# A depthwise-separable layer with k = 1: weights loaded in halves, a wait for each scaled slice, dummy matmuls, and a last store issued by two engines

## The chip, the core and the metric

The kernel runs on one core of a Trainium2 chip. The core has TensorE (matmuls into PSUM), VectorE, ScalarE, GpSimd and SyncE, and 16 DMA engines that move data between HBM and SBUF. In the profile they are called PE (with PEld for the loads of the stationary operand), DVE, ACT, POOL and SP; SPq and ACTq are the queues from which SyncE and ScalarE issue DMAs. The metric is device time in microseconds for one execution. About 0.2% can be told from no change.

## What is computed

```python
x: (1, 384, 384, 384), dw: (1, 1, 384), pw: (384, 384)      # bfloat16
out = x * dw[0, 0][None, None, None, :]                      # k = 1, pad = 0
return jnp.einsum('bhwc,cd->bhwd', out, pw)
```

With k = 1 the depthwise step is one factor for each channel. The kernel moves it into the weights: row c of pw is multiplied by dw[c] once, and all else is one matmul of 147,456 rows of 384 channels by a 384 x 384 matrix. x and the output are 113 MB each.

## The kernel before, in words

**Tiling.** Rows go through in 288 supertiles of 512. Supertiles are grouped in 76 chunks: 1, 1, 2, then 70 chunks of 4, then 2, 1, 1. A chunk of x is one load into one of four buffers X (1.5 MB for four supertiles); its output is one store from one of four buffers O. There are two buffers T for transposed data and two in PSUM (PS), for even and odd supertiles.

**One supertile.** VectorE transposes it from X to T with two 32-bit STREAM_TRANSPOSEs (line 174), half h = 0 for the channel blocks b = 0 to 2, h = 1 for b = 3 to 5. TensorE then runs 48 matmuls (line 134): six blocks b, two parities par, four row groups q of 32 rows each, which work side by side in the array; four matmuls with the same b and par make a "step". Each reads the scaled weights w_r of its slice (b, par) and accumulates into bank q. VectorE evicts bank 3 (line 212) and ScalarE banks 0 to 2 (line 215) to O as bfloat16, and VectorE transposes the supertile after the next.

**What sets the order.** Everything is written out by hand, with semaphores. Each engine runs its own instructions in order.

- SyncE issues, one after the other: the first x load, two loads of pw, the x loads of chunks 1 to 3; then in a loop over chunks t the load of chunk t + 4 (line 95; it waits until chunk t is transposed) and the store of chunk t (lines 105 and 107; they wait for both evictions). At the end it waits for all stores (line 125).
- ScalarE issues the load of dw and the two other loads of pw (line 89), loads its activation table, makes two tiny copies (line 160) that set s_a for the first turn, and then scales.
- pw is loaded four times, once into each group of 32 partitions: 288 KB each, 1.15 MB in all. dw becomes dwsel, one float factor for each partition, by four small copies on VectorE (line 186).
- Scaling: twelve slices (b, r) of 128 x 384; VectorE takes r = 0 (line 197), ScalarE r = 1 (line 199). Both wait for all four loads of pw. All twelve increment s_wr, and TensorE waits for twelve before its loop:

```python
        nc.tensor.wait_ge(s_wr, 2 * NB)
        with nc.tensor.Fori(0, NS // 2, 1) as it:
            rv = nc.tensor.to_reg(it + 1)
            for s in range(2):
                supertile(s, rv)
```

- The loop on TensorE is a hardware loop of 144 turns with two supertiles in its body. Inside, the first matmul of b = 0 and of b = 3 waits for the transposes (s_t), and matmuls of b = 0 wait for the evictions of the supertile that used this PSUM buffer (s_a at q = 0, s_d at q = 3).
- VectorE's order at the start is: seeds of s_d, dwsel, the transposes of supertile 0, its six slices, the transposes of supertile 1, then the loop of evictions and transposes.

Of the kernel before, what the change touches and what calls it, by code (L numbers as in the profile page):

```python
# [7 lines left out]
BF16 = mybir.dt.bfloat16  # L8
F32 = mybir.dt.float32
U32 = mybir.dt.uint32  # L10
COPY = mybir.ActivationFunctionType.Copy
# [3 lines left out]
NO = 4  # L15
# [11 lines left out]
def kernel(  # L27
# [11 lines left out]
    nc = tc.nc  # L39
    P = nc.NUM_PARTITIONS  # L40
    B, H, W, C = x.shape
    assert dw.shape[0] == 1 and dw.shape[1] == 1, "only k=1 depthwise supported"
    D = pw.shape[1]
    N = B * H * W
    assert C == 384 and D == 384 and N % 1024 == 0
    NB = C // 64

    xf = x.rearrange("b h w c -> (b h w) c")
    of = out.rearrange("b h w d -> (b h w) d")

    NS = N // 512
    chunks = _chunks(NS)
    NT = len(chunks)
    s0 = [sum(chunks[:t]) for t in range(NT)]

    consts = ctx.enter_context(tc.tile_pool(name="consts", bufs=1))
# [3 lines left out]
    pw_r = consts.tile([P, NB, 2, D], BF16, name="pw_r")  # L60
    w_r = consts.tile([P, NB, 2, D], BF16, name="w_r")
    dwt = consts.tile([32, NB, 2], BF16, name="dwt")
    dwsel = consts.tile([P, NB * 2], F32, name="dwsel")
    warm = consts.tile([P, 3], F32, name="warm")
    seed = consts.tile([P, 2], F32, name="seed")

    Xs = [bufp.tile([P, 4 * LMAX, C], BF16, name=f"X{i}") for i in range(NX)]
    Ts = [bufp.tile([P, NB, 256], BF16, name=f"T{i}") for i in range(2)]
    Os = [bufp.tile([P, 4 * LMAX * D], BF16, name=f"O{i}") for i in range(NO)]
    PS = [psum.tile([P, 4, 512], F32, name=f"ps{s}") for s in range(2)]  # L70
# [4 lines left out]
    s_a = [nc.alloc_semaphore(f"s_a{i}") for i in range(2)]  # L75
    s_d = [nc.alloc_semaphore(f"s_d{i}") for i in range(2)]
    s_o = [nc.alloc_semaphore(f"s_o{i}") for i in range(NO)]
    s_dw = nc.alloc_semaphore("s_dw")
    s_pw = nc.alloc_semaphore("s_pw")
    s_ds = nc.alloc_semaphore("s_ds")  # L80
    s_wr = nc.alloc_semaphore("s_wr")
    s_seed = nc.alloc_semaphore("s_seed")

    with tc.tile_critical():  # L84
        pw_v = pw.rearrange("(b w r) d -> w b (r d)", w=32, r=2)
        dw_v = dw.rearrange("a e (b w r) -> w (a e b) r", w=32, r=2)

        def load_pw(eng, q):
            eng.dma_start(pw_r[32 * q : 32 * q + 32].rearrange("w b r d -> w b (r d)"), pw_v).then_inc(s_pw, 16)  # L89

        def load_x(t):
            L = chunks[t]
            r = 512 * s0[t]
            src = xf[r : r + 512 * L, :].rearrange("(p s) c -> p (s c)", p=P)
            d = nc.sync.dma_start(Xs[t % NX][:, : 4 * L, :].rearrange("p s c -> p (s c)"), src)  # L95
            if t >= NX:
                je = s0[t - NX] + chunks[t - NX] - 1
                d._wait_ge(s_t[je % 2][1], je // 2 + 1)
            d.then_inc(s_x[t % NX], 16)

        def store(t):
            L = chunks[t]
            r = 512 * s0[t]
            je = s0[t] + L - 1
            nc.sync.wait_ge(s_d[je % 2], je // 2 + 2)
            dst = of[r : r + 512 * L, :].rearrange("(q p j) d -> p q (j d)", q=4, p=P)
            d = nc.sync.dma_start(dst, Os[t % NO][:, : 4 * L * D].rearrange("p (q e) -> p q e", q=4))
            d._wait_ge(s_a[je % 2], je // 2 + 2)
            d.then_inc(s_o[t % NO], 16)


        nc.scalar.dma_start(dwt[:], dw_v).then_inc(s_dw, 16)
        load_x(0)
        load_pw(nc.scalar, 2)
        load_pw(nc.sync, 0)
        load_pw(nc.scalar, 3)
        load_pw(nc.sync, 1)
        for t in range(1, NX):
            load_x(t)
        for t in range(NT):  # L120
            if t + NX < NT:
                load_x(t + NX)
            store(t)
        for o in range(NO):
            nc.sync.wait_ge(s_o[o], 16 * len(range(o, NT, NO)))


        def supertile(s, rv):
            for b in range(NB):
                for par in range(2):  # L130
                    for q in range(4):
                        if par == 0 and q == 0 and b in (0, 3):
                            nc.tensor.wait_ge(s_t[s][b // 3], rv)
                        mm = nc.tensor.matmul(  # L134
                            PS[s][:, q, :D],
                            lhsT=Ts[s][32 * q : 32 * q + 32, b, par::2],
                            rhs=w_r[32 * q : 32 * q + 32, b, par, :],
                            start=(b == 0 and par == 0),
                            stop=(b == NB - 1 and par == 1),
                            tile_position=(32 * q, 0),  # L140
                        )
                        if b == 0 and par == 0 and q == 0:
                            mm._wait_ge(s_a[s], rv)
                        elif b == 0 and par == 0 and q == 3:
                            mm._wait_ge(s_d[s], rv)
                        if b in (2, 5) and par == 1 and q == 3:
                            mm.then_inc(s_pe)

        nc.tensor.wait_ge(s_wr, 2 * NB)
        with nc.tensor.Fori(0, NS // 2, 1) as it:  # L150
            rv = nc.tensor.to_reg(it + 1)
            for s in range(2):
                supertile(s, rv)


        for s in range(2):
            nc.vector.memset(seed[:, s : s + 1], 0.0).then_inc(s_d[s])  # L157
        nc.gpsimd.memset(warm[:], 0.0).then_inc(s_seed)  # L158
        for s in range(2):
            c = nc.scalar.copy(warm[:, s + 1 : s + 2], warm[:, 0:1])  # L160
            if s == 0:
                c._wait_ge(s_seed, 1)
            c.then_inc(s_a[s])

        def transposes(t, j):
            jj = s0[t] + j
            L = chunks[t]
            s = jj % 2
            Xw = Xs[t % NX][:].bitcast(U32)[:, : 4 * L, :].rearrange("p (k l) c -> p k l c", l=L)
            Tw = Ts[s][:].bitcast(U32).rearrange("p b (i k) -> p b k i", k=4)  # L170
            for h in range(2):
                if h == 0 and j == 0:
                    nc.vector.wait_ge(s_x[t % NX], 16 * (t // NX + 1))
                ins = nc.vector.transpose(  # L174
                    out=Tw[:, 3 * h : 3 * h + 3],
                    in_=Xw[:, :, j, 96 * h : 96 * h + 96].rearrange("p k (b w) -> p b k w", w=32),
                )
                if jj >= 2:
                    ins._wait_ge(s_pe, 2 * (jj - 2) + h + 1)
                ins.then_inc(s_t[s][h])  # L180

        order = [(t, j) for t in range(NT) for j in range(chunks[t])]

        nc.vector.wait_ge(s_dw, 16)
        for q in range(4):
            nc.vector.tensor_copy(  # L186
                dwsel[32 * q : 32 * q + 32, :], dwt[:].rearrange("w b r -> w (b r)")
            ).then_inc(s_ds)
        transposes(*order[0])
        for b in range(NB):  # L190
            for r in range(2):
                eng = nc.vector if r == 0 else nc.scalar
                if b == 0:
                    eng.wait_ge(s_pw, 64)  # L194
                sc = dwsel[:, 2 * b + r : 2 * b + r + 1]
                if r == 0:
                    i = nc.vector.tensor_scalar_mul(w_r[:, b, r, :], pw_r[:, b, r, :], sc)  # L197
                else:
                    i = nc.scalar.activation(w_r[:, b, r, :], pw_r[:, b, r, :], COPY, scale=sc)  # L199
                if b == 0:  # L200
                    i._wait_ge(s_ds, 4)
                i.then_inc(s_wr)
        transposes(*order[1])

        for jj, (t, j) in enumerate(order):
            L = chunks[t]
            s = jj % 2
            Ov = Os[t % NO][:, : 4 * L * D].rearrange("p (q j d) -> p q j d", q=4, d=D)
            if j == 0 and t >= NO:
                nc.vector.wait_ge(s_o[t % NO], 16 * (t // NO))  # L210
                nc.scalar.wait_ge(s_o[t % NO], 16 * (t // NO))
            e = nc.vector.tensor_copy(Ov[:, 3, j, :], PS[s][:, 3, :D])  # L212
            e._wait_ge(s_pe, 2 * jj + 2)
            e.then_inc(s_d[s])
            a = nc.scalar.copy(Ov[:, 0:3, j, :], PS[s][:, 0:3, :D])  # L215
            a._wait_ge(s_pe, 2 * jj + 2)
            a.then_inc(s_a[s])
            if jj + 2 < NS:
                transposes(*order[jj + 2])


# [28 lines left out]
```

## Time and profile before

| | us |
|---|---|
| median of 9 runs (lowest, highest) | 587.65 (586.56, 588.87) |
| the profiled execution's own time | 587.25 |
| its span, first to last instruction | 585.5 |
| TensorE busy (L134), 13,824 matmuls | 564.2 |
| VectorE busy | 564.1 |
| ScalarE busy | 327.1 |
| DMA: 227.8 MB, mean rate over the span | 389 GB/s |

The costliest groups of instructions are below. The columns are line, engine, operation, output<-input, shapes, count, then busy us in all, mean ns of one, idle us of the engine just before them, and what ended most of it.

```profile
L134 PE MATMUL ps<-w_r,T 32*128 32x384 bf16 x13824 | 564.2, 322 | 12.8 <-ACT w_r L199 12.8
L215 ACT CAST O<-ps 128x1152 bf16<-128x1152 f32 x288 | 322.4, 1120 | 243.3 <-PE ps L134 243.3
L174 DVE STREAM_TRANSPOSE T<-X 128x384 uint32<-128x384 uint32 x576 | 448.7, 853 | 0.0
L212 DVE CAST O<-ps 128x384 bf16<-128x384 f32 x288 | 160.7, 558 | 6.4 <-PE ps L134 6.4
L199 ACT ACTIVATE w_r<-pw_r,dwsel 128x384 bf16<-128x384 bf16 x6 | 3.1, 601 | 5.4 <-DMA pw_r<-in_pw_dram 5.4
```

Four matmuls of a step overlap, so the mean of 322 ns is not the time between steps: a supertile takes 1.95 us, a step 0.1625 us. TensorE, VectorE and the DMA engines are all busy nearly throughout, and the page's shares don't tell which of them ends last. A time in a window is counted from the start of the span; in the windows' rows the numbers are the stretch, its length, busy us (and instructions) of PE, PEld, DVE, ACT and POOL, TensorE's granted clock, the mean busy share of the 16 DMA engines, and GB/s.

### The profile page before, as it was taken

Reading aid. Unit: us, or ns where it says so; the run is one execution under the profiler, and the core shown is the slowest. Engines: PE = TensorE matmul, PEld = TensorE weight load, DVE = VectorE, ACT = ScalarE, POOL = GpSimd, SP = SyncE. Lnnn points to the kernel's source line nnn. Section 1 sums busy time; section 2 is a strip of 40 time slices with the busy share of each in tenths; the row PEclk is TensorE's granted clock in tenths of the full one; section 3 lists DMA queues with packets and bytes.
Section 4 is the critical chain, followed back from the end, with each engine's and each line's share of the span. In section 5 each row is a group of like instructions: output and inputs, shape, how many; then the busy total and the mean of one; then the engine's idle time right before and its main releaser. Section 6 shows DMA issues by size and latency. Waiting matters only on the chain.

```text
span 585.5 us, 30055 instructions
## 1 busy us (share of the span) xinstructions
PE 564.2 (96%) x13824; PEld 385.4 (66%) x13824; DVE 564.1 (96%) x876; ACT 327.1 (56%) x297; POOL 0.3 (0%) x5
## 2 busy tenths in 40 slices
PE   1999999999999999999999999999999999999994
PEld 0666666666666666666666666666666666666662
DVE  3899999999999999999999999999999999999993
ACT  3455555555555555555555555555555555555553
POOL 0000000000000000000000000000000000000000
PEclk9999999999999999999999999999999999999998
DMA  8999999999999999999999999999999999999966
GB/s 296 344 410 408 409 400 383 401 406 418 404 396 389 394 418 419 400 403 400 404 397 401 411 407 399 391 412 413 401 384 404 405 401 400 401 401 399 374 239 223
DMA packets 52126, 227.81 MB, mean 389 GB/s; under 512 B 2704, under 2 KB 6544, under 8 KB 43152
## 3 DMA queue, kind: packets, MB, share of 16 engines
q1 hardware_dynamic: 51488, 227.09, 98.5%
q10 hardware_dynamic: 624, 0.59, 0.4%
q14 instruction: 13, 0.11, 0.0%
q8 instruction: 1, 0.02, 0.0%
HBM read 114.43 MB, written 113.25 MB: 389 GB/s over the span
## 4 chain that ended last, share of the span: by engine, by line
PE 96%; DMA 1%; ACT 1%; SPq 0%; issue 0%; ACTq 0%
PE ps L134 96%; DMA pw_r<-in_pw_dram 1%; ACT w_r L199 1%; ACT O L215 0%; SPq L89 0%; SPq L95 0%; SPq L245 0%; ACTq L194 0%; SPq L84 0%
## 5 line engine op out<-in xcount | busy, mean ns | idle before, releaser
L134 PE MATMUL ps<-w_r,T 32*128 32x384 bf16 x13824 | 564.2, 322 | 12.8 <-ACT w_r L199 12.8
L134 PEld LDWEIGHTS ps<-w_r,T 32*128 32x128 bf16 x13824 | 385.4, 93 | 191.2 <-issue 12.8
L215 ACT CAST O<-ps 128x1152 bf16<-128x1152 f32 x288 | 322.4, 1120 | 243.3 <-PE ps L134 243.3
L174 DVE STREAM_TRANSPOSE T<-X 128x384 uint32<-128x384 uint32 x576 | 448.7, 853 | 0.0
L212 DVE CAST O<-ps 128x384 bf16<-128x384 f32 x288 | 160.7, 558 | 6.4 <-PE ps L134 6.4
L199 ACT ACTIVATE w_r<-pw_r,dwsel 128x384 bf16<-128x384 bf16 x6 | 3.1, 601 | 5.4 <-DMA pw_r<-in_pw_dram 5.4
L186 DVE CAST dwsel<-dwt 32x12 f32<-32x12 bf16 x4 | 0.7, 163 | 3.5 <-DMA dwt<-in_dw_dram 3.4
L197 DVE TENSOR_SCALAR w_r<-pw_r,dwsel 128x384 bf16<-128x384 bf16 x6 | 1.5, 313 | 2.5 <-DMA pw_r<-in_pw_dram 2.5
L160 ACT ACT_TABLE_LOAD x1 | 1.3, 1283 | 2.3 <-issue 2.3
L157 DVE MEMSET seed<- 128x1 f32 x2 | 0.1, 59 | 1.0 <-SPq L84 1.0
L160 ACT COPY warm<-warm 128x1 f32<-128x1 f32 x2 | 0.3, 188 | 0.0
L234 POOL MEMSET const-bfloat16-1.0<- 128x1 bf16 x1 | 0.1, 102 | 0.0
L234 POOL MEMSET const-uint8-127<- 128x1 uint8 x1 | 0.1, 102 | 0.0
L158 POOL MEMSET warm<- 128x3 f32 x1 | 0.1, 101 | 0.5 <-SPq L84 0.5
L234 POOL MEMSET const-float32-1.0<- 128x1 f32 x1 | 0.1, 100 | 0.0
L234 POOL MEMSET const-float32-0.0<- 128x1 f32 x1 | 0.1, 99 | 0.2 <-issue 0.2
## 6 DMA issues: line engine op xcount, KB each, us to landing
X<-in_x_dram SPq DMA_DIRECT2D x70, 1536.0 KB, 13.0
out_dram<-O SPq DMA_DIRECT2D x70, 1536.0 KB, 14.5
X<-in_x_dram SPq DMA_DIRECT2D x4, 384.0 KB, 10.0
X<-in_x_dram SPq DMA_DIRECT2D x2, 768.0 KB, 13.3
out_dram<-O SPq DMA_DIRECT2D x4, 384.0 KB, 6.4
out_dram<-O SPq DMA_DIRECT2D x2, 768.0 KB, 8.5
pw_r<-in_pw_dram ACTq DMA_DIRECT2D x2, 288.0 KB, 5.8
pw_r<-in_pw_dram SPq DMA_DIRECT2D x2, 288.0 KB, 6.4
```

The costliest lines, as they stand in the source:

```text
L134: mm = nc.tensor.matmul(PS[s][:, q, :D], lhsT=Ts[s][32 * q : 32 * q + 32, b, par::2], rhs=w_r[32 * q : 32 * q + 32, b, par, :], start=(b = ...
L157: nc.vector.memset(seed[:, s : s + 1], 0.0).then_inc(s_d[s])
L158: nc.gpsimd.memset(warm[:], 0.0).then_inc(s_seed)
L160: c = nc.scalar.copy(warm[:, s + 1 : s + 2], warm[:, 0:1])
L174: ins = nc.vector.transpose(out=Tw[:, 3 * h : 3 * h + 3], in_=Xw[:, :, j, 96 * h : 96 * h + 96].rearrange("p k (b w) -> p b k w", w=32),)
L186: nc.vector.tensor_copy(dwsel[32 * q : 32 * q + 32, :], dwt[:].rearrange("w b r -> w (b r)")).then_inc(s_ds)
L197: i = nc.vector.tensor_scalar_mul(w_r[:, b, r, :], pw_r[:, b, r, :], sc)
L199: i = nc.scalar.activation(w_r[:, b, r, :], pw_r[:, b, r, :], COPY, scale=sc)
L212: e = nc.vector.tensor_copy(Ov[:, 3, j, :], PS[s][:, 3, :D])
L215: a = nc.scalar.copy(Ov[:, 0:3, j, :], PS[s][:, 0:3, :D])
L234: nc = _bacc.Bacc("TRN2", target_bir_lowering=False, num_devices=1)
```

## The change

1. Each of the four loads of pw becomes two, for the blocks b = 0 to 2 and 3 to 5, with a semaphore for each half. All first halves are issued before the second halves.
2. ScalarE makes dwsel instead of VectorE. Of the twelve slices VectorE scales nine and ScalarE three ((0,1), (2,1), (4,1)). An engine waits for the second half of pw only ahead of its first slice of b = 3 or more.
3. TensorE no longer waits for all slices before its loop. In the even supertile of the loop body the first matmul (q = 0) of each slice but the first waits for that slice; the first is waited for once, ahead of the loop. These waits stay in the loop for all its turns.
4. GpSimd clears a tile `zero`, and TensorE runs 14 matmuls on it into the odd PSUM buffer before it waits for the first slice.
5. In the last supertile VectorE and ScalarE evict two banks each, and its store is issued in two halves, by SyncE after VectorE's eviction and by ScalarE after its own.

```diff
-        def load_pw(eng, q):
-            eng.dma_start(pw_r[32 * q : 32 * q + 32].rearrange("w b r d -> w b (r d)"), pw_v).then_inc(s_pw, 16)
+        def load_pw(eng, q, h):
+            bs = slice(3 * h, 3 * h + 3)
+            eng.dma_start(
+                pw_r[32 * q : 32 * q + 32, bs].rearrange("w b r d -> w b (r d)"), pw_v[:, bs]
+            ).then_inc(s_pw[h], 16)
...
         load_x(0)
-        load_pw(nc.scalar, 2)
-        load_pw(nc.sync, 0)
-        load_pw(nc.scalar, 3)
-        load_pw(nc.sync, 1)
+        for h in range(2):
+            for q in range(2):
+                load_pw(nc.scalar, 2 + q, h)
+                load_pw(nc.sync, q, h)
         for t in range(1, NX):
             load_x(t)
-        for t in range(NT):
+        for t in range(NT - 1):
             if t + NX < NT:
                 load_x(t + NX)
             store(t)
+        o_last = Os[(NT - 1) % NO][:, : 4 * D].rearrange("p (q e) -> p q e", q=4)
+        of_last = of[N - 512 :, :].rearrange("(q p) d -> p q d", p=P)
+        nc.sync.dma_start(of_last[:, 2:4], o_last[:, 2:4])._wait_ge(s_d[(NS - 1) % 2], (NS - 1) // 2 + 2).then_inc(
+            s_last, 16
+        )
...
+        wr_eng = {(b, r): int(r == 1 and b % 2 == 0) for b in range(NB) for r in range(2)}
...
                         if b == 0 and par == 0 and q == 0:
                             mm._wait_ge(s_a[s], rv)
+                        elif s == 0 and q == 0:
+                            mm._wait_ge(*wr_done[b, par])
...
-        nc.tensor.wait_ge(s_wr, 2 * NB)
+        nc.tensor.wait_ge(s_zero, 1)
+        for i in range(14):
+            nc.tensor.matmul(
+                PS[1][:, i % 4, :D],
+                lhsT=zero[32 * (i % 4) : 32 * (i % 4) + 32, 0:P],
+                rhs=zero[32 * (i % 4) : 32 * (i % 4) + 32, :],
+                start=True,
+                stop=True,
+                tile_position=(32 * (i % 4), 0),
+            )
+        nc.tensor.wait_ge(*wr_done[0, 0])
...
+        nc.gpsimd.memset(zero[:].bitcast(U32), 0).then_inc(s_zero)
...
-        nc.vector.wait_ge(s_dw, 16)
+        nc.scalar.wait_ge(s_dw, 16)
         for q in range(4):
-            nc.vector.tensor_copy(
-                dwsel[32 * q : 32 * q + 32, :], dwt[:].rearrange("w b r -> w (b r)")
-            ).then_inc(s_ds)
+            nc.scalar.copy(dwsel[32 * q : 32 * q + 32, :], dwt[:].rearrange("w b r -> w (b r)")).then_inc(s_ds)
         transposes(*order[0])
...
+        first = {}
+        for (b, r), e in wr_eng.items():
+            eng = (nc.vector, nc.scalar)[e]
+            if (e, b // 3) not in first:
+                eng.wait_ge(s_pw[b // 3], 64)
+            sc = dwsel[:, 2 * b + r : 2 * b + r + 1]
+            if e == 0:
+                i = nc.vector.tensor_scalar_mul(w_r[:, b, r, :], pw_r[:, b, r, :], sc)
+            else:
+                i = nc.scalar.activation(w_r[:, b, r, :], pw_r[:, b, r, :], COPY, scale=sc)
...
+            first[e, b // 3] = True
+            i.then_inc(s_wr[e])
         transposes(*order[1])
...
-            e = nc.vector.tensor_copy(Ov[:, 3, j, :], PS[s][:, 3, :D])
+            nq = 3 if jj + 1 < NS else 2
+            e = nc.vector.tensor_copy(Ov[:, nq:4, j, :], PS[s][:, nq:4, :D])
...
-            a = nc.scalar.copy(Ov[:, 0:3, j, :], PS[s][:, 0:3, :D])
+            a = nc.scalar.copy(Ov[:, 0:nq, j, :], PS[s][:, 0:nq, :D])
...
+        nc.scalar.dma_start(of_last[:, 0:2], o_last[:, 0:2])._wait_ge(s_a[(NS - 1) % 2], (NS - 1) // 2 + 2).then_inc(
+            s_last, 16
+        )
```

More of the change, by code (lines that the diff above doesn't have):

```diff
@@ L65 @@
     seed = consts.tile([P, 2], F32, name="seed")
+    zero = consts.tile([P, D], BF16, name="zero")
     Xs = [bufp.tile([P, 4 * LMAX, C], BF16, name=f"X{i}") for i in range(NX)]
@@ L78 @@
     s_dw = nc.alloc_semaphore("s_dw")
-    s_pw = nc.alloc_semaphore("s_pw")
+    s_pw = [nc.alloc_semaphore(f"s_pw{h}") for h in range(2)]
     s_ds = nc.alloc_semaphore("s_ds")
-    s_wr = nc.alloc_semaphore("s_wr")
+    s_wr = [nc.alloc_semaphore(f"s_wr{e}") for e in range(2)]
     s_seed = nc.alloc_semaphore("s_seed")
+    s_zero = nc.alloc_semaphore("s_zero")
+    s_last = nc.alloc_semaphore("s_last")
     with tc.tile_critical():
@@ L123 @@
             store(t)
-        for o in range(NO):
-            nc.sync.wait_ge(s_o[o], 16 * len(range(o, NT, NO)))
+        o_last = Os[(NT - 1) % NO][:, : 4 * D].rearrange("p (q e) -> p q e", q=4)
[3 more added lines that the diff above has]
+        )
+        for o in range(NO):
+            nc.sync.wait_ge(s_o[o], 16 * len(range(o, NT - 1, NO)))
+        nc.sync.wait_ge(s_last, 32)
+        wr_eng = {(b, r): int(r == 1 and b % 2 == 0) for b in range(NB) for r in range(2)}
+        wr_done, made = {}, [0, 0]
+        for k, e in wr_eng.items():
+            made[e] += 1
+            wr_done[k] = (s_wr[e], made[e])
         def supertile(s, rv):
@@ L182 @@
         order = [(t, j) for t in range(NT) for j in range(chunks[t])]
-        nc.vector.wait_ge(s_dw, 16)
+        nc.scalar.wait_ge(s_dw, 16)
         for q in range(4):
-            nc.vector.tensor_copy(
-                dwsel[32 * q : 32 * q + 32, :], dwt[:].rearrange("w b r -> w (b r)")
-            ).then_inc(s_ds)
+            nc.scalar.copy(dwsel[32 * q : 32 * q + 32, :], dwt[:].rearrange("w b r -> w (b r)")).then_inc(s_ds)
         transposes(*order[0])
[L190 to L202, printed above, removed]
+        first = {}
[8 more added lines that the diff above has]
+                i = nc.scalar.activation(w_r[:, b, r, :], pw_r[:, b, r, :], COPY, scale=sc)
+            if (e, b // 3) not in first and b == 0:
+                i._wait_ge(s_ds, 4)
+            first[e, b // 3] = True
+            i.then_inc(s_wr[e])
         transposes(*order[1])
```

## The prediction

> **What bounds the kernel.** I read the chain of waits first. In order of time (start us, us, what) its end pieces are
>
> ```profile
> 1.88 7.34 DMA pw_r<-in_pw_dram
> 9.22 0.02 issue
> 9.24 0.02 ACTq L194
> 9.26 0.05 issue
> 9.31 3.15 ACT w_r L199 x6
> 12.46 0.32 issue
> 12.78 564.23 PE ps L134 x13161
> 577.01 0.02 issue
> 577.04 1.12 ACT O L215
> ```
>
> TensorE works without a gap from 12.78 to 577.01; before it stand the loads of pw and six scalings on ScalarE. Read alone, this says that each microsecond taken from the head is won. But the chain stops at the last eviction, at 578.2, and the span is 585.5. I looked at what fills those 7.3 us, in the windows at the end (mean granted clock, DMA share and GB/s are the last three columns):
>
> ```profile
> 579.00:580.00 1.00, 0.00 (x0) 0.00 (x0) 0.00 (x0) 0.00 (x0) 0.00 (x0) 1.00 0.83 290
> 580.00:581.00 1.00, 0.00 (x0) 0.00 (x0) 0.00 (x0) 0.00 (x0) 0.00 (x0) 0.98 0.37 128
> 581.00:582.00 1.00, 0.00 (x0) 0.00 (x0) 0.00 (x0) 0.00 (x0) 0.00 (x0) 0.50 0.07 24
> 582.00:583.00 1.00, 0.00 (x0) 0.00 (x0) 0.00 (x0) 0.00 (x0) 0.00 (x0) 0.50 0.07 23
> ```
>
> A share of 0.07 is one DMA engine of sixteen (1/16 = 0.063). Fifteen have landed their part by about 580.7; one works alone until 583.8. The last store, issued at 578.18, lands 5.9 us later, at 584.1, and the exit takes 1.4 us more. That engine is late from long before. The landing times of the X loads (us from issue, min/median/max) in the stretches 30 to 70, 250 to 290 and 500 to 540 us are
>
> ```profile
> DMA to landing us min/median/max: 8.3/8.4/8.7
> DMA to landing us min/median/max: 12.8/13.0/13.3
> DMA to landing us min/median/max: 18.7/19.0/19.3
> ```
>
> A landing is that of its slowest engine. It slips by 19.0 - 8.4 = 10.6 us in about 60 chunks of four supertiles: 0.177 us a chunk. TensorE takes 4 x 1.95 = 7.80 us a chunk, so the slow engine takes 7.97: it is never idle and never catches up. VectorE doesn't feel it, since a load is issued three chunks (23.4 us) ahead of its use. **Two chains run beside each other**: TensorE, from 12.78 at 1.95 us a supertile, and one DMA engine, which gets its bytes from the first load on. The second ends last, by 584.1 - 580.7 = 3.4 us. Its end can only move by idle time that it still has. In the windows at the start:
>
> ```profile
> 18.00:20.00 2.00, 2.00 (x56) 1.39 (x52) 1.55 (x4) 0.66 (x1) 0.00 (x0) 1.00 0.70 242
> 20.00:22.00 2.00, 2.00 (x56) 1.37 (x52) 2.00 (x4) 1.17 (x2) 0.00 (x0) 1.00 0.77 190
> 22.00:24.00 2.00, 2.00 (x57) 1.35 (x49) 2.00 (x4) 1.17 (x2) 0.00 (x0) 1.00 1.01 369
> 24.00:26.00 2.00, 2.00 (x56) 1.39 (x52) 2.00 (x4) 1.17 (x2) 0.00 (x0) 1.00 0.89 294
> ```
>
> The DMA engines had been full (1.0) from 4 us on with X0 to X4 and pw; at 18.8 they run dry, because the first store comes only at 18.0 and the sixth load at 18.45, and these hang on the first supertile's matmuls.
>
> **Head, TensorE's side.** The eight half loads carry the same bytes as the four loads. Two of those had landed at 1.35 + 5.0 = 6.3 and 1.40 + 5.4 = 6.8, all four at 9.2. So the first halves (as many bytes as those two) should be there at 6.8, the second at 9.2. SP and ACT each issue two more (0.42 to 0.46 us a piece in the rows of L89); X1 to X3 on SP are issued 0.9 us later, behind bytes that are still flowing at 8.2: nothing. ACT's table load ends at about 4.5 instead of 3.6, its warm copies at 4.8; the four dwsel copies moved to it (VectorE's took 163 ns, ACT's tiny copy 188) end at 5.6, with 1.2 us of cover before 6.8; uncovered they would cost 0.75. VectorE, freed of them, transposes X0 when it lands (0.95 + 3.8 = 4.8) until 6.4.
>
> Then scaling: VectorE takes nine slices (313 ns each, 229 apart), ACT three (599). First-half slices: 6.9 to 8.0. TensorE starts at 7.2 instead of 12.78. Second half: five slices on VectorE from 9.3, the last done at 9.3 + 4 x 0.229 + 0.31 = 10.5; supertile 0 done at 10.9, before at 16.86. VectorE transposes X1 (there at 9.95) from 10.3 to 11.85, so supertile 1 starts at 11.1. Cold, a step of four matmuls takes 0.32 us against 0.1625 warm; before, the cold steps end 4.8 us after the first matmul. Cold throughout, supertile 1 ends at 15.0 (before 19.34); warm from the start it would end at 13.1. Warmth comes somewhere between: TensorE gains 3 to 6 us; I take 4.7. The **dummies** (14, or 3.5 cold steps = 1.1 us, from about 1.5 us) are over by 3; they are far shorter than the 4.8 us that warming took, and 4 us of idleness follow. I give them nothing, and no cost: TensorE has no other work then. The memset of their zeros has L158's 0.10 us as its nearest row; even 1 us is hidden.
>
> **Per-slice waits.** Eleven matmuls of every even supertile carry a wait for a slice, in all 288/2 x 11 = 1584, satisfied after the first turn. TensorE's queue stands behind each. Nearest rows: the matmuls that now carry satisfied waits (s_a, s_d, s_t). Across them the step stays at 0.162 to 0.163 us, as elsewhere, and all matmuls of L134 between 40 and 60 us last 321 ns at least, in the middle and at most. Cost 0; upper end 1 ns each, 1.6 us. The separate s_t wait at b = 3 is like the one already at b = 0 (51 ns, step unchanged). TensorE has 3.4 us of room now and more after its earlier start.
>
> **Tail.** The last eviction is split two and two. ACT's half falls between 747 (two thirds of 1120) and 1120 ns, VectorE's between 558 and 1116; taking 0.85 and 1.0, the later is 0.1 us earlier than now. The last store is issued half by SP and half by ACT, about 0.37 us each in parallel. Against it speaks the Trainium skill ("DMA: Bandwidth & Descriptors", section "Issuing engines are not separate DMA queues"): DMAs of all issuing engines share the same 16 DMA engines, and concurrent issue saves only issue time. The trace has no split store, but pw from two queues: all four land by 9.2 with the engines at 1.05 to 1.10 busy, so two queues were not faster. By the row nearest to the end (the slow engine's remaining bytes) the tail gains 0; if issue and eviction counted, 0.1 to 0.5. I take 0.
>
> **The sum.** With TensorE earlier by 3 us or more, store 0 is issued near 12.8, the sixth load near 13, the second store near 15.5: all before X4's data ends at 18.8, so the idle hole closes. Its size from two sides. From shares: (1.02 - 0.70, 0.77, 1.01, 0.89) x 2 us = 0.64 + 0.50 + 0.02 + 0.26 = 1.4. From landings: X4 lands at 6.9 + 12.3 = 19.2, the load issued at 29.2 lands at 37.1; between lie two chunks' worth of bytes, 2 x 7.97 = 15.9 of 17.9 us: 2.0. I take 1.9. Four more completions cost 9 ns each on that engine: nothing. So span 585.5 - 1.9 = 583.6 and profiled 587.25 - 1.9 = 585.35. The median of the runs, 587.65, is 0.4 above the profiled one: **585.7 us**, 0.3% faster, though TensorE starts 5.6 us sooner.
>
> Here a second rule weighs: the same page ("Latency and other measured facts") says that DMA engines 7 and 15 are usually slower, puts it as a guess down to descriptor rings of GpSimd's queue, and excludes queues such as SP's. Nearly all of this trace's traffic is on such queues (q1 and q10, both hardware_dynamic), and still one engine lags. By the rule's cause all sixteen would be even and TensorE's 4.7 us would count; by the windows 1.9. I go by the windows.
>
> **Rivals.**
> TensorE's start decides after all (14%). For it: the chain of waits names only TensorE. Against: the lone engine at the end. It needs a slow engine that lags less in the timed runs. Gain 4.7 + 0.1: 582.9.
> The hole isn't closed, or is paid back (14%): the dip at 24 to 26 us came with work queued, so it may not be lack of requests, and X5's issue took 1.5 us on SP. Gain under 1: 587.2.
> Slower (10%): a wait on a slice keeps its weight load from being pulled ahead of the running matmul. It decides only where TensorE loses more than its own lead: 584.1 less (580.7 - 4.8) = 8.2 us, or 5.2 ns for each of 1584. At 20 ns (one matmul's share of a weight-load slot, 1.95/96) it costs 31.7, so 587.65 + 31.7 - 8.2 = 611. The equal steps across today's waits speak against it; for it, that no supertile today has eleven such waits in a row.
> The forecast has the remaining 62%. Its own range is 584.4 to 586.4: the hole 1.3 to 2.9 (the upper end if the slow engine also runs its longer solo end faster: its last L = 4 store took 3.9 instead of 4.3 us).
>
> **Numbers.** About 0.2% (1.2 us) can be told from no change here. Faster: 55 of the 62 plus 14 = 69%; same: 7 + 14 = 21%; slower 10%. The range 582.6 to 587.6 takes in the first two rivals and leaves out the third.
>
> **What would show it.** First slice matmul near 7.2, TensorE's end near 572.3; DMA share without the dip at 18 to 26; X landings at 500 to 540 grown from 19.0 to about 21.8 (TensorE is 4.7 earlier, the slow engine 1.9); a share of 0.06 to 0.07 at the end for about 6 us instead of 3. I am wrong if that lone stretch doesn't lengthen, or if steps of L134 in even supertiles exceed 0.163 us.

## The result, and the profile after

| | before | after |
|---|---|---|
| median (us), lowest to highest | 588.22 (586.56 to 591.02, 31 runs) | 584.80 (583.92 to 585.74, 10 runs) |
| ratio after/before, 95% interval | | 0.9943 (0.9930 to 0.9956) |
| profiled execution: own time, span | 587.25, 585.5 | 588.49, 586.7 |
| TensorE's first matmul on real data | 12.8 | 7.9 |
| supertile 1 done (its eviction starts) | 19.34 | 14.23 |

The change makes the kernel 3.4 us faster (2.6 to 4.1 by the interval), while TensorE is ahead by 19.34 - 14.23 = 5.1 us after two supertiles. The profiled execution of the changed kernel is slower than any of the ten in this median (the record lists three more outside the ten, at 584.83, 586.64 and 588.93), so it shows where things happen, not how long the kernel takes.

The chain of waits of the changed kernel (start us, us, what), cut to its long pieces and to one of its turns:

```profile
7.14 0.03 issue
7.17 0.02 DVEq L225
7.19 0.05 issue
7.25 0.56 DVE w_r L228 x2
7.81 0.10 issue
7.90 493.80 PE ps L153 x11509
501.71 0.02 issue
501.73 1.13 ACT O L248
502.86 0.02 issue
502.87 25.18 DMA out_dram<-O
...
530.14 23.30 DMA out_dram<-O
```

Up to 501 us it is the chain of before, begun 4.9 us earlier. Then a store holds it for 25 us, and another for 23: evictions now wait for a buffer O, and the engines stand still at times. TensorE's lead is given back there: its last matmul ends at 576.9, before at 577.0. The landing times of the X loads, in the stretches 30 to 70, 250 to 290 and 500 to 540 us as before (8.4, 13.0 and 19.0 in the middle), and in the last line SP's issues of the loads of the third stretch (ns min/median/max):

```profile
DMA to landing us min/median/max: 11.1/11.2/11.4
DMA to landing us min/median/max: 15.5/15.9/16.3
DMA to landing us min/median/max: 23.9/25.1/25.9
L101 SPq DMA_DIRECT2D X<-in_x_dram x5: 327/5130/6761, 499.9 to 532.0; - x5
```

TensorE is earlier, the slow DMA engine is less so, and the distance between them is larger from the start: 11.2 instead of 8.4. At the end it is the whole lead that three chunks of buffers allow (23.4 us), and SP itself is held up: an issue that takes 0.33 us takes up to 6.8. The windows at the start, where the hole was (the two columns before the last number of each row are the clock and the DMA share, then GB/s):

```profile
18.00:20.00 2.00, 2.00 (x56) 1.18 (x52) 2.00 (x4) 1.12 (x1) 0.00 (x0) 1.00 1.07 403
20.00:22.00 2.00, 2.00 (x60) 1.19 (x52) 2.00 (x4) 1.12 (x1) 0.00 (x0) 1.00 1.04 439
22.00:24.00 2.00, 2.00 (x56) 1.22 (x52) 2.00 (x5) 1.14 (x2) 0.00 (x0) 1.00 0.90 359
24.00:26.00 2.00, 2.00 (x56) 1.19 (x52) 2.00 (x5) 1.17 (x2) 0.00 (x0) 1.00 1.11 445
```

The shares of 0.70 and 0.77 have become 1.07 and 1.04, and the mean rate of these four rows is 411 GB/s instead of 274. And at the end one engine still works alone, for 4 us where it was 3:

```profile
581.00:582.00 1.00, 0.00 (x0) 0.00 (x0) 0.00 (x0) 0.00 (x0) 0.00 (x0) 0.50 0.07 26
582.00:583.00 1.00, 0.00 (x0) 0.00 (x0) 0.00 (x0) 0.00 (x0) 0.00 (x0) 0.50 0.07 25
583.00:584.00 1.00, 0.00 (x0) 0.00 (x0) 0.00 (x0) 0.00 (x0) 0.00 (x0) 0.50 0.07 23
584.00:585.00 1.00, 0.00 (x0) 0.00 (x0) 0.00 (x0) 0.00 (x0) 0.00 (x0) 0.50 0.07 23
```

### The profile page after: what moved, and what is told of

It reads as the page before. It is cut to its first block, busy times and chain, and to the rows that moved or that the text cites. A ratio compares the mean times of both kernels' runs of the same rounds, so it can differ in the third digit from the quotient of the medians.

```text
span 586.7 us, 30232 instructions
## 1 busy us (share of the span) xinstructions
PE 566.8 (97%) x13838; PEld 342.4 (58%) x13838; DVE 563.7 (96%) x875; ACT 326.0 (56%) x298; POOL 0.5 (0%) x6
## 4 chain that ended last, share of the span: by engine, by line
PE 84%; DMA 12%; DVE 1%; SPq 1%; ACT 1%; issue 0%; DVEq 0%; ACTq 0%
PE ps L153 84%; DMA out_dram<-O 11%; DMA pw_r<-in_pw_dram 1%; SPq L101 1%; ACT O L248 1%; DVE T L207 1%; DVE O L245 0%; DVE w_r L228 0%; SPq L93 0%; DVEq L242 0%; SPq L281 0%; DVEq L225 0%; SPq L111 0%; ACTq L243 0%; SPq L87 0%
## 5 line engine op out<-in xcount | busy, mean ns | idle before, releaser
L153 PEld LDWEIGHTS ps<-w_r,T 32*128 32x128 bf16 x13824 | 341.9, 93 | 232.5 <-issue 9.7
L230 ACT ACTIVATE w_r<-pw_r,dwsel 128x384 bf16<-128x384 bf16 x3 | 1.7, 610 | 2.7 <-DMA pw_r<-in_pw_dram 2.7
L173 PE MATMUL ps<-zero 32*128 32x384 bf16 x14 | 1.5, 515 | 1.3 <-POOL zero L191 1.3
## 6 DMA issues: line engine op xcount, KB each, us to landing
X<-in_x_dram SPq DMA_DIRECT2D x4, 384.0 KB, 11.6
X<-in_x_dram SPq DMA_DIRECT2D x2, 768.0 KB, 15.4
```

What stands on the lines that cost most here:

```text
L153: mm = nc.tensor.matmul(PS[s][:, q, :D], lhsT=Ts[s][32 * q : 32 * q + 32, b, par::2], rhs=w_r[32 * q : 32 * q + 32, b, par, :], start=(b = ...
L173: nc.tensor.matmul(PS[1][:, i % 4, :D], lhsT=zero[32 * (i % 4) : 32 * (i % 4) + 32, 0:P], rhs=zero[32 * (i % 4) : 32 * (i % 4) + 32, :], s ...
```

## The experiments

Theory D: one slow DMA engine ends last, and only idle time of that engine is worth anything. Theory P: in the timed runs TensorE's chain ends last, and the profiles mislead. All medians are beside runs of the kernel before on the same chip (588.4 to 588.7 in the middle).

**More work for TensorE.** Four small matmuls more in each turn of the changed kernel's loop, adding zeros:

```diff
+                if s == 1 and b == 1:
+                    for q in range(4):
+                        nc.tensor.matmul(
+                            PS[s][:, q, 0:64],
+                            lhsT=zero[32 * q : 32 * q + 32, 0:P],
+                            rhs=zero[32 * q : 32 * q + 32, 0:64],
+                            start=False,
+                            stop=False,
+                            tile_position=(32 * q, 0),
+                        )
```

> The changed kernel with four more matmuls of 64 columns (zeros added to zeros' effect on the sums) in each of the 144 turns of TensorE's loop. By their columns they are a sixth of a step, 0.027 us, so TensorE's work grows by 3.9 us, and by up to 7 if their weight loads show. Theory D (one slow DMA engine ends last, TensorE has some 6 to 8 us of room): the time stays that of the changed kernel, about 3.3 us under the kernel before, at most 1 us more. Theory P (in the timed runs TensorE's chain ends last): the changed kernel's time plus 4 to 7 us, so 0.6 to 4 us above the kernel before.

Measured: 585.67 us, ratio 0.9952 (0.9937 to 0.9966), 0.9 us above the changed kernel (0.5 by the ratios, whose intervals overlap). The chain of this kernel shows turns as pieces of their own:

```profile
507.77 3.90 PE ps L153 x96
511.70 3.90 PE ps L153 x96
```

A turn takes 511.70 - 507.77 = 3.93 us (3.90 before; the trace's steps give 0.0295 more), so TensorE has 144 x 0.0295 = 4.2 us more to do. The kernel pays a small part of it. P wanted all of it and falls.

**One wait for all slices.** The per-slice waits of the change undone:

```diff
-                        elif s == 0 and q == 0:
-                            mm._wait_ge(*wr_done[b, par])
...
-        nc.tensor.wait_ge(*wr_done[0, 0])
+        nc.tensor.wait_ge(s_wr[0], 9)
+        nc.tensor.wait_ge(s_wr[1], 3)
```

> The changed kernel with the per-slice waits undone: TensorE waits once for all twelve slices ahead of its loop, none inside. Its first real matmul moves from 7.9 to about 10.7 us, supertile 0's end from 12.0 to about 14.5, and all of TensorE's work by some 2.3 us. D: no change against the changed kernel (3.3 us under the kernel before, within 0.5), since store 0 and the sixth load are still issued before the DMA engines run dry at 18.8. P: about 1 us under the kernel before.

Measured: 585.00 us, 0.9944 (0.9926 to 0.9962). Its chain of waits has

```profile
11.02 563.87 PE ps L153 x13333
574.89 0.02 issue
574.92 0.96 DVE O L244
```

TensorE begins 3.1 us later than in the changed kernel and the time is 0.2 longer, which can't be told from nothing. The eleven waits in each turn neither cost nor bring anything that shows within the 1 us of these intervals. In the changed kernel's trace the steps of even supertiles, which carry the waits, are 0.162 to 0.163 us, like those of the odd ones.

**Each half alone.** The last supertile's part of the change on the kernel before, and the changed kernel without it:

```diff
+            nq = 3 if jj + 1 < NS else 2
-            e = nc.vector.tensor_copy(Ov[:, 3, j, :], PS[s][:, 3, :D])
+            e = nc.vector.tensor_copy(Ov[:, nq:4, j, :], PS[s][:, nq:4, :D])
...
-        for t in range(NT):
+        for t in range(NT - 1):
```

> The kernel before with the change's last supertile alone: evictions two and two, last store in halves from two engines. D: no difference that can be measured (0, within 0.3 us). P: 0.3 to 0.5 us faster.

> The changed kernel with the last supertile as before, so only the start differs from the kernel before. D: the whole gain, about 3.3 us under the kernel before. P: 2.8 to 3.0 us under it.

Measured: the tail alone 588.21, 1.0001 (0.9987 to 1.0015); the head alone 585.17, 0.9943 (0.9922 to 0.9964). The gain is the head's. The intervals (0.8 us and more to each side) are too wide to tell 0 from P's 0.3 to 0.5. What the split does is seen in the changed kernel's profile, in the stores of the last supertile (issues by engine, then us to landing):

```profile
L253 ACTq DMA_DIRECT2D out_dram<-O x1: 485/485/485, 578.6 to 578.6; - x1
L132 SPq DMA_DIRECT2D out_dram<-O x1: 372/372/372, 578.7 to 578.7; - x1
...
DMA to landing us min/median/max: 2.5/4.6/6.6
```

ACT's half lands after 2.5 us, past everything that still stands in SP's queue of the slow engine; SP's half after 6.6, at 585.4. In the profile of the head alone the whole store, issued by SP at 579.1, landed at 585.6: the split did not bring the end forward.

**No dummies.** The 14 matmuls, their zeros and their wait left out of the changed kernel:

```diff
-        nc.tensor.wait_ge(s_zero, 1)
-        for i in range(14):
...
```

> The changed kernel without the 14 dummy matmuls, the cleared tile and their wait. TensorE's steps were still 0.32 us when the real matmuls began at 7.9, so the dummies had not warmed it; at most the warming at 12.1 comes some 1 to 3 us later and TensorE's chain with it. D: no change against the changed kernel (3.3 us under the kernel before, within 0.5), as TensorE's chain has room. P: 0 to 1.5 us slower than the changed kernel.

Measured: 584.90, 0.9941 (0.9917 to 0.9964), against 584.80 with them. In this profile the granted clock rose and the steps became short (0.16 us instead of 0.32) at 13.6, in the changed kernel's at 12.3, and supertile 1 was done at 14.90 instead of 14.23: one execution each, 0.7 us of TensorE's time, none of the kernel's that shows.

**The hole closed without the change.** If D is right, TensorE need not start earlier at all: it is enough to have the sixth load queued in time. One digit of the kernel before:

```diff
-NX = 4
+NX = 5
```

> The kernel before with five X buffers instead of four and nothing else: the sixth x load is issued with the first ones and no longer waits for the first supertile. TensorE starts when it did (12.8 us). D: the DMA engines no longer run dry at 18.8 us, so the slow engine, and with it the kernel, gains most of what the change gained: 2 to 3.3 us. P: 0, since TensorE starts and runs as before.

Measured: 585.37, 0.9946 (0.9926 to 0.9966). Its windows:

```profile
18.00:20.00 2.00, 2.00 (x44) 1.27 (x40) 1.02 (x3) 0.12 (x2) 0.00 (x0) 1.00 0.99 418
20.00:22.00 2.00, 2.00 (x57) 1.35 (x49) 2.00 (x4) 1.17 (x2) 0.00 (x0) 1.00 1.01 420
```

TensorE starts at 12.87, as before; the DMA engines don't run dry; the gain, 3.2 us by the medians, is that of the whole change. (The fifth buffer also puts every later load one chunk further ahead of its use; TensorE's start it leaves alone.)

**Which engine.** Small loads of k = 1 to 15 partitions, meant to take k descriptors on k of the engines:

```diff
+            k = t - 50
+            if 1 <= k <= 15:
+                nc.sync.dma_start(probe[k][0:k, :], xf[0:k, :]).then_inc(s_probe[k], 16)
```

> The kernel before with fifteen tiny loads put among the others on SP, one in each of chunks 51 to 65: the k-th has k partitions of 768 bytes and so k descriptors, one for each of k DMA engines. D: up to some k they land with the quick engines (some 8 to 11 us after issue), from that k on with the slow one (17 to 19 us), and k tells which of the sixteen it is. If instead no single engine is slow but all are late together, the latency doesn't jump with k. The time is that of the kernel before, within 1 us.

Measured: 587.54 (one run). The trace has k completions for each (and one more update when the issue ends). The latest came after 6.8, 7.4, 7.5 and 9.8 us for k = 1 to 4, after 16.9 for k = 5, and after 17.1 to 19.5 from there on, with one late completion each and all others within 6.6 to 11.3. It is the engine that gets the fifth share. The X loads of the kernel before, which have 16 completions each, show a single late one too: from the load issued at 131 us to that at 521, the 15th came 9 to 11 us after the issue, and only the last grew, from 9.9 to 19.0. SP's issues of k = 4 and k = 5 show the jump too:

```profile
L128 SPq DMA_DIRECT2D probe<-in_x_dram x1: 406/406/406, 431.1 to 431.1; - x1
L128 SPq DMA_DIRECT2D probe<-in_x_dram x1: 1873/1873/1873, 438.9 to 438.9; - x1
```

**Help for the slow engine.** Longer descriptors and larger buffers, with and without the change:

```diff
-LMAX = 4
+LMAX = 8
...
-NO = 4
+NO = 3
...
-    head, tail = [1, 1, 2], [2, 1, 1]
+    head, tail = [1, 1, 2, 4], [4, 2, 1, 1]
```

> The changed kernel with chunks of eight supertiles in the middle (and of four at both ends), three O buffers instead of four. A store's descriptors grow from 3072 to 6144 bytes. In the kernel before the slow engine needed 4.26 us for its 32 descriptors of 3072 bytes and 3.7 for the same bytes of a load in 12288; the early load in 6144 took 240 ns a descriptor, 16 x 0.24 = 3.84 us for those bytes. So the slow engine falls to about 7.55 us for four supertiles, under TensorE's 7.80. D: it keeps pace, TensorE's chain ends last, and its earlier start comes out in full: 578.5 to 580 us, 8 to 10 under the kernel before. P (or a slow engine that doesn't gain by longer descriptors): the changed kernel's time, 584 to 586.

> The kernel before with the same chunks and O buffers, without the change. D: with the slow engine keeping pace, TensorE's chain from 12.8 us on ends last, about 583.5 to 585 us; beside the run with the change this gives what the change is worth where TensorE decides: about 5 us instead of 3.3. If the slow engine doesn't gain by longer descriptors: 585 to 588, and the difference between the two stays below 3.5 us.

Measured: with the change 585.37, 0.9954 (0.9936 to 0.9971): missed by 5 us. Without it 584.55, 0.9933 (0.9913 to 0.9953): as expected. The waits of the first name the cause:

```profile
DVE O L245 <- DMA out_dram<-O: 4.9, 1, 4.9
```

One wait of 4.9 us: the fifth supertile's buffer O (the first again, with three) was still to be stored by store 0, which stood behind a load of eight supertiles until 25.1 us. TensorE stood still, and after it its granted clock was halved from 26.4 to 29.8 us. My design took back just what the change had won. With three X and four O buffers and chunks that grow more slowly (LMAX = 8 stays):

```diff
-NX = 4
+NX = 3
...
-    head, tail = [1, 1, 2], [2, 1, 1]
+    head, tail = [1, 1, 2, 4, 4], [4, 4, 2, 1, 1]
```

> As the changed kernel with chunks of eight (label after_l8), whose profile lost 5 us near the start: the fifth supertile's eviction waited for the first store of its O buffer until 25.1 us, because with three O buffers that was store 0, queued behind a load of eight supertiles. Here three X buffers and four O buffers, and the chunks grow more slowly (1, 1, 2, 4, 4, then 33 of 8, then 4, 4, 2, 1, 1). D: that wait is gone, the slow engine keeps pace, TensorE's chain ends last from its earlier start: 578.5 to 580.5 us, 8 to 10 under the kernel before. If the slow engine still sets the end: 584 to 586.

Measured: **580.42 us**, 0.9869 (0.9848 to 0.9889), faster than both. Its chain and its end:

```profile
7.89 564.83 PE ps L153 x11758
572.73 0.02 issue
572.75 0.96 DVE O L245
```

```profile
575.00:576.00 1.00, 0.00 (x0) 0.00 (x0) 0.00 (x0) 0.00 (x0) 0.00 (x0) 1.00 0.83 277
576.00:577.00 1.00, 0.00 (x0) 0.00 (x0) 0.00 (x0) 0.00 (x0) 0.00 (x0) 0.96 0.07 25
577.00:578.00 1.00, 0.00 (x0) 0.00 (x0) 0.00 (x0) 0.00 (x0) 0.00 (x0) 0.50 0.01 5
```

Nothing holds TensorE from 7.89 to 572.7, and the lone engine works 1.2 us at the end instead of 3 to 4. The time came where I expected it, but not for the reason in its size: X loads, now of eight supertiles, land 14.7 us after issue at 30 to 70 us and 19.7 at 480 to 502, so the engine still slips by about 5 us in 28 chunks, 0.09 for four supertiles instead of 0.18, not the gain of 0.42 that I had worked out. It catches up in the last 60 us. The packets' own times say why the gain in its pace was small: in the median, 3072 bytes took 121 ns and 6144 took 234, 12288 took 460 and 24576 took 912. An engine's 32 store packets and 8 load packets for four supertiles come to 7.55 us, and half as many twice as long to 7.39: 0.16 less, an estimate from medians over all engines. How much of the kernel's gain is the longer descriptors and how much the larger buffers was not separated.

**The same two questions where the slow engine doesn't decide.** The four small matmuls, and the kernel before, with these chunks:

> The four more matmuls of 64 columns in each turn (as in label pe_more, where they added 0.0295 us to a turn and 4.2 us to TensorE's work, but 0.9 us to the time) on top of the chunks of label after_l8b. D: with the slow engine keeping pace the same 4.2 us now count in full: 580.4 + 4.2 = 584.6 us, within 0.7. P, or anything in which TensorE's work doesn't decide here: 580.4 to 582.

> The kernel before with the chunks of label after_l8b: beside that run it gives what the change is worth where TensorE decides. From the two profiles TensorE is 5.1 us earlier by the change, and the split tail can give 0.2 more. D: 585 to 586 us, 4.5 to 5.3 above after_l8b. If the change's worth is bounded by something else also here: 583.5 to 584, the 3.3 us of the first comparison.

Measured: 582.81 and 585.02. The change is worth 4.6 us here, as expected, against 3.4 in the plain kernel. TensorE's 4.2 us of added work cost 2.4, between the two answers: more than 0.9, not all. In the profiles TensorE's last eviction came 3.0 us later rather than 4.2, because its granted clock rose earlier in that execution (at 11.6 instead of 13.7 us, and supertile 1 took 2.0 us instead of 2.9); the lone engine's 1.2 us may have hidden another part. So D holds in direction, and with these chunks the two chains end nearly together.

## Why the prediction came out right

**What ends last** was the prediction's main step, and it held in the timed runs: 4.2 us more for TensorE cost 0.9 or less (pe_more), a start 3.1 us later cost 0.2 (one_wait), and the gain can be had without touching TensorE's start (before_nx5). The rival in which TensorE's start decides gave 582.9 and is out, and so is the one in which the hole isn't closed. Of the two signs of being wrong that the prediction names, slower steps in even supertiles did not come. The other came near: the lone stretch was to grow from 3 to about 6 us and grew to 4 in the changed kernel's profile, because TensorE, held at the O buffers, ended at 576.9 and not at 572.3.

**The hole** was the term that was mis-sized: 1.9 us in the sum, 3.4 measured, 3.2 with the hole closed alone. Both of its counts came out small.

- The first went by the mean busy share of the engines, 1.4 us. The last column of the same rows says more: between 18 and 26 us, 411 GB/s in the changed kernel against 274 are 1.1 MB that were not moved, or 2.7 us at the changed kernel's rate (an estimate).
- The second allowed the slow engine two average chunks, 15.9 us, between the landings at 19.2 and 37.1. What stood in its queue there was loads for 12 supertiles and stores for 4. At the 3.7 and 4.26 us for four supertiles that the expectation of after_l8 works out, these take 15.4, which leaves 2.5.

The load of chunk 20, in the kernel before and in the changed one (issue, then us to landing):

```profile
L95 SPq DMA_DIRECT2D X<-in_x_dram x1: 328/328/328, 130.6 to 130.6; - x1
...
DMA to landing us min/median/max: 9.9/9.9/9.9
```

```profile
L101 SPq DMA_DIRECT2D X<-in_x_dram x1: 328/328/328, 125.5 to 125.5; - x1
...
DMA to landing us min/median/max: 12.4/12.4/12.4
```

It landed at 140.5 before and at 137.9 after. The kernels that start as before (before, tail_only, probes) had it at 140.5 to 140.8, those with the change's head (after, head_only, pe_more, no_dummies, and one_wait with its later start) at 137.5 to 138.3: 2.8 us between the middles, and still 2.7 at chunk 30. So the later lead is what the bytes of the hole give. The 0.6 us between 2.8 and 3.4 lie inside the interval and are not accounted for.

Landings alone mislead at the edge of the hole: the load of chunk 7 seems only 37.1 - 35.7 = 1.4 us earlier in the changed kernel. But of its 16 completions the first 15 had come by 37.0 before and by 34.6 after, 2.4 apart, and a single one came 1.1 us later than these. That single one is late from the load of chunk 4 on, just after a lone packet of 16,384 bytes on the instruction queue q8 that took 1.07 us at 15.5. In the kernel before the same packet went at 18.5, into the hole. That it held this engine is likely, but packets don't name their engine.

**Luck** had a part in the time. A gain of 3.4 us lies above the prediction's own 1.3 to 2.9. The time lies inside its 584.4 to 586.4 because the kernel before had a median of 588.22 in the comparison and not the 587.65 of the sum, from which the same gain leads to 584.2.

**The head** on TensorE's side: first halves of pw at 7.1 (6.8 predicted), first matmul 7.9 (7.2), second halves 9.5 (9.2), supertile 0 done at 12.0 (10.9), supertile 1 at 14.2 (between 13.1 and 15.0), lead 5.1 us (4.7). Each time was a little late and the warming a little early. The bounds of 13.1 and 15.0 for supertile 1 are a gain of 4.3 to 6.2 us, not of 3 to 6 as the prediction has it.

**Waits, dummies, tail at nothing:** one_wait and no_dummies stay within 0.2 us of the changed kernel, and tail_only shows no difference. The rule of the Trainium skill that the prediction cites ("DMA: Bandwidth & Descriptors", "Issuing engines are not separate DMA queues"), that DMAs of all issuing engines share the 16 DMA engines, fits what the split store did. That all sixteen engines would be even, which the prediction weighed and set aside, is out: every profile has a late one. The equal steps of 0.162 us across the waits of the kernel before had been enough to set the slower case aside.

**The lag** was to grow to 21.8 us; in the profiles shown it was 25.1 in the changed kernel and 21.7 without the dummies. What the prediction didn't see is that at about 23 us the lag reaches the buffers' lead and stops TensorE. In the profiled execution the slow engine lost time there, too. Its loads had landed about 7.94 us apart; from chunk 60 to 70 eight of eleven came 8.3 to 8.8 after the one before. It was 2.6 us ahead of the kernel before at chunk 50 (377.2 against 379.8) and 1.7 behind at chunk 70 (541.3 against 539.6), which is why this execution was not faster. Its loads were issued some 20 to 25 us ahead, so a want of requests is unlikely; the cause is open. The ten timed runs, 3.4 us faster in the middle, cannot have lost all of it.

## What to carry to other kernels

Follow the last store to its landing before you trust a chain that ends at the last eviction: here a DMA share of 1/16 at the end, and landing times that grew through the run by one completion of sixteen, said that one DMA engine was the bound. Then an earlier start of the compute is worth only the idle time that it takes out of that engine, and a fifth load buffer (one digit) did as much as the whole change. Size that idle time by the bytes that were not moved, not by the mean busy share of the engines (2.7 us against 1.4 here). With chunks twice as long, where the slow engine all but kept pace, the same earlier start was worth 4.6 us instead of 3.4.

## What the hardware showed that I had not expected

- One of the 16 DMA engines took 7.97 us for what the others did within TensorE's 7.80, with nearly all traffic on SP's queue. Every profile has one such late completion in its X loads, 5.7 us or more behind the other fifteen between 470 and 530 us, on each of the four chips that the record names. That it is the engine with the fifth share is known from the probes alone, on one chip. Why is open.
- SP's issue of a DMA is held when that engine is far behind: 0.36 to 0.42 us for probes of up to four descriptors, 1.9 to 4.9 for the larger ones, and up to 6.8 for x loads when the lag was 25 us.
- A half store on ACT's queue landed in 2.5 us while the slow engine still had older stores in SP's queue that landed at up to 584.8. The second queue overtook; it didn't shorten the whole.
- Profiled executions of kernels with a long lag were longer than their timed medians (588.49 against 584.80, 588.72 against 585.17 for the head alone, 588.43 against 585.37 for before_nx5), others were not (584.52 against 585.00 for one_wait). Whether the recording slows the slow engine was not tried.
